# A new order of all steps, and four products with k on GpSimd, in a fused linear-attention and SwiGLU kernel

## The chip, the core and the metric

The kernel runs on one core of one Trainium2 chip. The metric is the device time of one execution in microseconds (us). One profiled execution gives the trace that the numbers below are from.

## What is computed

The first half is a linear attention with a decaying state (RWKV-6), for 4 batches, 8 heads, 768 time steps and head dimension 48; the second a feed-forward part on its output, 3072 rows of 384, with 1536 hidden units.

```
for t in range(S):
    cur = einsum('bhd,bhe->bhde', u * k[t], v[t])
    y[t] = einsum('bhd,bhde->bhe', r[t], state + cur)
    state = w[t][..., None] * state + einsum('bhd,bhe->bhde', k[t], v[t])
x  = y as rows (batch, time) of 384
xn = x / sqrt(mean(x * x) + 1e-6) * rms_g
g  = xn @ w_gate
out = (g * sigmoid(g) * (xn @ w_val)) @ w_out
```

## The kernel before

Time is cut into six blocks n of 128 steps, with four batches j. The order is written out by hand: ORDER is a list of steps `name.n.j`, and the last loop calls the function of each name in that order. Every engine executes its own instructions in the order in which they were called, so ORDER sets the order on TensorE, VectorE, ScalarE, GpSimd and SP's DMA queue at once. What a step waits for on other engines is found from its data.

For a block and a batch, load_w, load_k, load_r and load_v bring 128 x 384 values (L261, SP's queue). ln takes the logarithm of w (ScalarE); cs_mm, for blocks 0 and 1 pcs_mm, adds it up over time with a triangular matrix (TensorE); exp_r and exp_k make exponentials (ScalarE); r_mul and k_mul multiply r and k with them into rk (L471, L477); rk_pe or a DMA transposes it to rkT (rk_tr). q_mm (L518, L520) or pq_mm (L529, L531) multiply r with k, masks cut away the future (q_mask, pmask: VectorE, or a copy by ScalarE and a select by GpSimd), y_mm multiplies with v, st_mm (L575) and st_new bring the state on. The term with u runs on the side: bonus_mul (GpSimd, L483 and L484) makes r k u, bonus_sum (VectorE) its sum per head, bonus_v (GpSimd, L493) times v gives ydiag. x_add adds both. x_sq (ScalarE), x_rstd (GpSimd or ScalarE) and xn_mul (ScalarE, L624) normalize, xn_pe or xn_tr transpose, xn_out multiplies with rms_g.

The feed-forward part takes 512 rows at a time. Blocks 0 and 1 go together as pairs: pgate and pval (L670) work on 256 rows, first those of batch 0, then of batch 1; gate_mm.1 and val_mm.1 (L663) on batches 2 and 3 of the two blocks; gate_mm.2 to gate_mm.5 on blocks 2 to 5 of all batches. A feed-forward group is six matmuls of 256 columns or three of 512; a Silu (ScalarE, table loads at L236) and a product (VectorE) follow it, then o_mm (L720) and out_dma.

The weights w_gate and w_val come in three pieces each, w_out in three: load_gv.g.h (L367; h is 0 for gate, wg_sb_154 to 156 for g of 0 to 2; 1 for val, wv_sb_157 to 159) and load_wo. GpSimd issues them, in its own list between its products, on queue 0 of the DMA; loads of w, k, r and v are on SP's queue 1. pgate.f.0 for f of 0 and 1 uses piece 0, for 2 and 3 piece 1, for 4 and 5 piece 2. PSUM has rings: a and b with two banks each, q with four.

A few sets say which engine does a step: K_POOL (k_mul on GpSimd), CAST_ACT (the cast of v on ScalarE), ODD_COPY (the second mask by ScalarE and GpSimd, not VectorE), RSTD_ACT, EXPR_SB and EXPK_SB (exponentials into SBUF, not PSUM). warm steps are products of zeros on TensorE.

Of the kernel before, what the change touches and what calls it, by code (L numbers as in the profile page):

```python
# [30 lines left out]
pcopy_o.0.0 k_mul.0.1 warm.1.2 rk_pe.0.1 load_w.0.2 ln.0.2 exp_k.1.1 pcs_mm.1.2 load_w.0.3 ln.0.3 pcs_mm.2.2 r_mul.1.1
pmask_e.0.0 k_mul.1.1 rk_pe.1.1 pmask_o.0.0 pmask_o.2.0 pmask_e.2.0 exp_r.1.2 pcs_mm.0.2 exp_k.1.2 load_k.0.2
bonus_sum.1.1 k_mul.1.2 cast_v.0.0 y_mm.1.0 pmask_o.1.0 bonus_v.1.0 x_add.1.0 rk_tr.1.1 load_k.0.3 load_v.0.1
bonus_v.0.0 exp_k.0.2 k_mul.0.2 y_mm.0.0 warm.3.1 x_add.0.0 rk_tr.0.1 pq_mm.3.1 warm.2.2 pcopy_o.3.1 pmask_e.3.1
pq_mm.2.1 pmask_o.2.1 pmask_e.2.1 pcs_mm.1.3 x_sq.1.0 pq_mm.1.1 warm.0.1 x_sq.0.0 load_r.0.2 exp_r.0.2 w_tot.0.2
r_mul.0.2 load_gv.1.0 x_rstd.1.0 pq_mm.0.1 pmask_o.0.1 pmask_e.0.1 pmask_e.1.1 pmask_o.1.1 x_rstd.0.0 bonus_mul.0.1
pmask_o.3.1 load_gv.1.1 xn_mul.1.0 exp_r.1.3 bonus_v.1.1 cast_v.0.1 pcs_mm.0.3 pcs_mm.2.3 rk_pe.0.2 load_gv.0.0
xn_pe.1.0 xn_out.1.0 load_gv.0.1 bonus_sum.0.1 exp_k.1.3 xn_mul.0.0 warm.2.1 xn_pe.0.0 bonus_v.0.1 rk_tr.0.2
xn_out.0.0 y_mm.1.1 x_add.1.1 exp_k.0.3 y_mm.0.1 load_w.2.1 ln.2.1 exp_r.0.3 st_mm.0.1 st_new.0.1 r_mul.1.2 pgate.3.0
st_mm.0.0 st_new.0.0 psilu.3.0 pgate.2.0 psilu.2.0 load_gv.2.0 load_r.0.3 k_mul.0.3 x_add.0.1 r_mul.0.3 x_sq.1.1  # L40
# [10 lines left out]
cs_add.2.1 x_rstd.1.2 pmask_o.1.3 pmask_o.2.3 ln.2.2 xn_mul.1.2 o_mm.0.1 load_w.2.3 load_k.2.0 load_r.2.3 ln.2.0
cs_mm.2.0 x_rstd.0.2 bonus_v.0.3 exp_k.2.1 cs_add.2.0 pmask_o.0.3 exp_k.2.0 bonus_sum.1.3 o_out.0.1 y_mm.0.3 pval.5.1
ph.5.1 pmask_o.3.3 exp_r.2.1 y_mm.1.3 k_mul.2.0 bonus_v.1.3 x_add.0.3 st_mm.0.2 st_new.0.2 load_r.2.1 r_mul.2.1
w_tot.2.1 xn_mul.0.2 x_add.1.3 ln.2.3 exp_r.2.0 w_tot.2.0 o_mm.0.3 xn_pe.0.2 xn_pe.1.2 x_sq.0.3 x_rstd.0.3 o_out.0.3
cs_mm.2.3 xn_out.0.2 cs_add.2.3 load_r.2.0 r_mul.2.0 o_mm.0.0 load_k.2.3 xn_out.1.2 bonus_mul.2.3 load_k.2.1 k_mul.2.1
load_w.3.0 x_sq.1.3 x_rstd.1.3 xn_mul.1.3 load_r.2.2 xn_mul.0.3 load_w.3.1 exp_r.2.3 xn_pe.1.3 cs_mm.2.2 cs_add.2.2
exp_r.2.2 load_v.2.3 exp_k.2.2 rk_tr.2.0 out_dma.0.1 rk_tr.2.1 xn_out.1.3 xn_pe.0.3 xn_out.0.3 load_k.2.2 r_mul.2.2
w_tot.2.2 o_mm.0.2 ln.3.0 exp_k.2.3 r_mul.2.3 w_tot.2.3 ln.3.1 load_v.2.1 val_mm.1.4 gate_mm.1.8 gate_mm.1.3 st_mm.0.3
silu.1.8 o_out.0.0 bonus_mul.2.1 o_out.0.2 silu.1.3 bonus_sum.2.1 st_new.0.3 val_mm.1.8 h_mul.1.8 gate_mm.1.4 silu.1.4
h_mul.1.4 q_mm.2.0 q_mask_e.2.0 q_copy_o.2.0 q_copy_o.2.1 bonus_mul.2.0 cast_v.2.3 k_mul.2.3 q_mask_e.2.1 k_mul.2.2  # L60
# [70 lines left out]
def kernel(  # L131
# [646 lines left out]
```

## Time and profile before

| | us |
|---|---|
| median of 3 runs | 201.34 |
| lowest and highest | 200.47 and 202.33 |
| the profiled execution | 202.45 |
| its span, first to last instruction | 200.6 |
| TensorE's last matmul ends at | 197.3 |

Times in a view count from the first instruction of the span. PE is TensorE, PEld its weight load, DVE VectorE, ACT ScalarE, POOL GpSimd; SPq and POOLq are an engine's sequencer, which issues DMAs. A row of a timeline gives start, duration, engine, line, operation, out<-in and count, and behind `<-` what ended the idle time ahead of it. A row of waits gives the total, the number of waits and the longest one. Durations of successive rows overlap, since engines are pipelined.

### The profile page before, as it was taken

To read this page: it belongs to the slowest core of one execution; us is meant where nothing else is said; L and a number is where in the kernel's file an instruction comes from. 1 tells how busy PE (TensorE), PEld (TensorE's weight loads), DVE (VectorE), ACT (ScalarE), POOL (GpSimd) and SP (SyncE) were. 2 spreads that over 40 slices of the span, in tenths; PEclk is the share of its full clock that TensorE was granted. 3 is DMA by queue.
4 is the path that set the end of the run, shared out by engine and by line. 5 is a ranking of instruction groups with operands and counts; after the bars stand their busy time and mean duration, and the time that the engine had idled before them with its cause. 6 is when DMAs were issued, how large, how long until landed. Compare 5 with 4: busy or idle time off the path is not lost.

```text
span 200.6 us, 4665 instructions
## 1 busy us (share of the span) xinstructions
PE 190.2 (95%) x1708; PEld 120.3 (60%) x1724; DVE 150.6 (75%) x298; ACT 138.9 (69%) x282; POOL 129.3 (64%) x191
## 2 busy tenths in 40 slices
PE   7989968999999989999899999999999999999993
PEld 3556667998765556565456665565655655555562
DVE  5699986979986999998888887798698682154631
ACT  3699996778889448987568986579976665064400
POOL 3599959797399957798879997937696742000000
PEclk9999999999999999999999999999999999999999
DMA  6999999999969899899999768896276002302222
GB/s 160 323 323 233 229 203 194 216 196 212 191 149 203 182 189 207 207 195 180 157 232 202 149 179 177 168 224 132 44 186 141 3 2 59 98 3 78 78 78 78
DMA packets 109886, 32.41 MB, mean 162 GB/s; under 512 B 103972, under 2 KB 109480, under 8 KB 109864
## 3 DMA queue, kind: packets, MB, share of 16 engines
q1 hardware_dynamic: 107024, 28.58, 63.8%
q0 software_dynamic: 2832, 3.54, 10.3%
q8 instruction: 13, 0.21, 0.4%
q14 instruction: 9, 0.07, 0.1%
q10 hardware_dynamic: 8, 0.00, 0.0%
HBM read 25.96 MB, written 4.72 MB: 153 GB/s over the span
## 4 chain that ended last, share of the span: by engine, by line
PE 66%; POOL 13%; DMA 12%; issue 3%; ACT 2%; DVE 1%; SPq 1%; POOLq 0%; DVEq 0%
PE ps_bv L663 8%; PE ps_bu L663 8%; PE ps_au L663 7%; PE ps_av L663 7%; PE ps_qv L720 6%; PE ps_qx L720 5%; PE ps_qu L720 5%; DMA wv_sb<-in_moe_w_val_dram 5%; DMA rkT<-rk 5%; POOL ruk L483 3%; POOL ruk L484 2%; PE ps_qz L720 2%; POOL rk L477 2%; DMA stage_v<-in_v_dram 2%; PE ps_bu L670 2%
## 5 line engine op out<-in xcount | busy, mean ns | idle before, releaser
L720 PEld LDWEIGHTS <-ht 128*128 128x128 bf16 x300 | 28.4, 98 | 17.4 <-DVE ht L706 0.3
L238 ACT ACTIVATE sg<-ps_au 128x512 bf16<-128x512 f32 x35 | 21.0, 599 | 17.2 <-PE ps_au L663 12.9
L238 ACT ACTIVATE sg<-ps_av 128x512 bf16<-128x512 f32 x37 | 22.1, 599 | 12.9 <-PE ps_av L663 10.7
L706 DVE TENSOR_TENSOR ht<-ps_bv,sg 128x512 bf16<-128x512 f32 x30 | 20.6, 687 | 11.5 <-PE ps_bv L663 8.8
L663 PEld LDWEIGHTS <-wg_sb 128*128 128x128 bf16 x180 | 19.3, 114 | 15.8 <-DVE xnt L652 0.2
L663 PEld LDWEIGHTS <-wv_sb 128*128 128x128 bf16 x180 | 19.0, 114 | 15.3 <-DVE xnt L652 0.2
L483 POOL TENSOR_TENSOR ruk<-stage_r,stage_k 128x384 f32<-128x384 f32 x24 | 24.0, 1001 | 4.5 <-DMA stage_r<-in_r_dram 4.4
L484 POOL TENSOR_TENSOR ruk<-ruk,u_bc 128x384 f32<-128x384 f32 x24 | 24.2, 1007 | 2.2 <-POOL ruk L483 0.4
L663 PE MATMUL ps_av<-xnt,wg_sb 128*128 128x512 bf16 x89 | 25.0, 380 | 0.2
L706 DVE TENSOR_TENSOR ht<-ps_bu,sg 128x512 bf16<-128x512 f32 x30 | 20.6, 688 | 5.6 <-PE ps_bu L663 2.9
L663 PE MATMUL ps_bv<-xnt,wv_sb 128*128 128x512 bf16 x85 | 24.1, 380 | 0.3
L663 PE MATMUL ps_bu<-xnt,wv_sb 128*128 128x512 bf16 x86 | 23.9, 380 | 0.4 <-issue 0.2
L663 PE MATMUL ps_au<-xnt,wg_sb 128*128 128x512 bf16 x84 | 23.3, 380 | 0.1
L493 POOL TENSOR_TENSOR ydiag<-stage_v,diag 128x384 f32<-128x384 f32 x24 | 19.8, 832 | 2.0 <-DVE wcol L466 1.0
L477 POOL TENSOR_TENSOR rk<-stage_k,ek 128x384 bf16<-128x384 f32 x16 | 15.9, 1004 | 6.0 <-ACT ek L238 6.0
L720 PE MATMUL ps_qv<-wo_sb,ht 128*128 128x384 bf16 x108 | 19.1, 326 | 0.0
L611 ACT ACTIVATE junk<-xb 128x384 bf16<-128x384 f32 x24 | 12.5, 523 | 5.8 <-DVE xb L606 5.6
L559 POOL TENSOR_SCALAR_AFFINE_SELECT qts<-qts 128x512 bf16<-128x512 bf16 x16 | 10.1, 635 | 8.1 <-ACT qts L556 8.1
L624 ACT ACTIVATE xn<-xb,rstd 128x384 bf16<-128x384 f32 x24 | 14.4, 610 | 1.0 <-POOL rstd L620 0.9
L236 ACT ACT_TABLE_LOAD x10 | 12.8, 1283 | 1.8 <-PEq L762 1.6
L720 PE MATMUL ps_qu<-wo_sb,ht 128*128 128x384 bf16 (+1 forms) x84 | 13.8, 314 | 0.0
L488 DVE TENSOR_REDUCE diag<-ruk 128x8 f32<-128x384 f32 x24 | 13.1, 544 | 0.4 <-POOL ruk L484 0.3
(216 smaller groups left out, 413.5 us busy)
## 6 DMA issues: line engine op xcount, KB each, us to landing
out_dram<-ob SPq DMA_DIRECT2D x23, 192.0 KB, 2.2
stage_w<-in_w_dram SPq DMA_DIRECT2D x16, 192.0 KB, 4.1
stage_k<-in_k_dram SPq DMA_DIRECT2D x16, 192.0 KB, 3.7
stage_r<-in_r_dram SPq DMA_DIRECT2D x16, 192.0 KB, 4.2
stage_v<-in_v_dram SPq DMA_DIRECT2D x16, 192.0 KB, 3.9
stage_w<-in_w_dram SPq DMA_DIRECT2D x4, 384.0 KB, 4.9
stage_k<-in_k_dram SPq DMA_DIRECT2D x4, 384.0 KB, 5.5
stage_r<-in_r_dram SPq DMA_DIRECT2D x4, 384.0 KB, 4.9
```

Of the source, the lines that this page charges most:

```text
L236: nc.scalar.preload_act_table_set(table_name)
L238: return nc.scalar.activation(**kw).ins
L477: eng.tensor_tensor(out=rk[:, n % 2, j, 1, :, 0:D], in0=inp["k", n, j], in1=bank["ek", n, j][:, 0:DM].rearrange("p (h d) -> p h d", h=H), ...
L483: nc.gpsimd.tensor_tensor(out=ruk[n, j], in0=inp["r", n, j], in1=inp["k", n, j], op=ALU.mult)
L484: nc.gpsimd.tensor_tensor(out=ruk[n, j], in0=ruk[n, j], in1=u_bc, op=ALU.mult)
L488: nc.vector.tensor_reduce(out=diag[n, j].rearrange("p h o -> p (h o)"), in_=ruk[n, j], axis=mybir.AxisListType.X, op=ALU.add)
L493: nc.gpsimd.tensor_tensor(out=ydiag[n, j], in0=inp["v", n, j], in1=diag[n, j].to_broadcast([128, H, D]), op=ALU.mult)
L611: nc.scalar.activation(out=junk, in_=xb[n, j], func=AF.Square, accum_out=rstd[n, j][:, 0:1])
L624: nc.scalar.activation(out=xn, in_=xb[n, j], func=AF.Copy, scale=rstd[n, j][:, 1:2])
L663: nc.tensor.matmul(ps, lhsT=units(ws, c, f), rhs=xnt[n][:, c, :], start=(c == 0), stop=(c == KC - 1))
L706: nc.vector.tensor_tensor(out=ht[n][:, f, :], in0=bank.pop(("v", n, f)), in1=bank.pop(("sg", n, f)), op=ALU.mult)
L720: nc.tensor.matmul(ps[:, cols], lhsT=ht[n][:, f, b * L:(b + 1) * L], rhs=wo_sb[:, f, cols], start=(f == 0), stop=(f == FC - 1))
```

## The change

ORDER is another list of the same steps; 9 warm steps where there were 8. Five sets differ. The rest is the same, one line higher up in the file.

```diff
-load_w.0.0 gain_mm.0.0 ln.0.0 pcs_mm.2.0 exp_k.1.0 load_k.0.0 k_mul.1.0 pcs_mm.1.0 u_mm.0.0 exp_r.1.0 exp_k.0.0
+load_w.0.0 ln.0.0 pcs_mm.2.0 exp_k.1.0 load_k.0.0 k_mul.1.0 load_r.0.0 pcs_mm.1.0 exp_r.1.0 r_mul.1.0 u_mm.0.0
...
-    CAST_ACT = sel("02")
-    EXPR_SB = sel("03 13")
-    K_POOL = sel("20 21 22 23 30 31 32 33 40 41 42 43 50 51 52 53")
-    EXPK_SB = sel("13") | K_POOL
+    CAST_ACT = sel("01 02 03")
+    EXPR_SB = sel("02 03 13")
+    K_POOL = sel("02 03 12 13 20 21 22 23 30 31 32 33 40 41 42 43 50 51 52 53")
+    EXPK_SB = K_POOL
...
-    ODD_COPY = sel("00 02 03 10 12 31 32 33")
-    RSTD_ACT = sel("00 02 10 13")
+    ODD_COPY = sel("00 03 12 22 23 32 33")
+    RSTD_ACT = sel("00 10")
```

GpSimd's list around the issues of the weights, before (ydiag is bonus_v, the two lines of ruk are one bonus_mul, CAST vp is cast_v, rstd is x_rstd):

```order
L493 TENSOR_TENSOR ydiag<-stage_v,diag 128x384 x2
L367 DMA wg_sb_155<-in_moe_w_gate_dram 128x3x512
L483 TENSOR_TENSOR ruk<-stage_r,stage_k 128x384
L484 TENSOR_TENSOR ruk<-ruk,u_bc 128x384
L547 AFFINE_SELECT qts<-qts 128x512
L367 DMA wv_sb_158<-in_moe_w_val_dram 128x3x512
L493 TENSOR_TENSOR ydiag<-stage_v,diag 128x384
L408 CAST vp<-stage_v 128x768
L367 DMA wg_sb_154<-in_moe_w_gate_dram 128x3x512
L367 DMA wv_sb_157<-in_moe_w_val_dram 128x3x512
L493 TENSOR_TENSOR ydiag<-stage_v,diag 128x384
L367 DMA wg_sb_156<-in_moe_w_gate_dram 128x3x512
```

The same place now, which begins behind two bonus_mul:

```order
L366 DMA wg_sb_154<-in_moe_w_gate_dram 128x3x512
L482 TENSOR_TENSOR ruk<-stage_r,stage_k 128x384
L483 TENSOR_TENSOR ruk<-ruk,u_bc 128x384
L407 CAST vp<-stage_v 128x768
L546 AFFINE_SELECT qts<-qts 128x512
L492 TENSOR_TENSOR ydiag<-stage_v,diag 128x384 x2
L366 DMA wv_sb_157<-in_moe_w_val_dram 128x3x512
L366 DMA wg_sb_155<-in_moe_w_gate_dram 128x3x512
L366 DMA wv_sb_158<-in_moe_w_val_dram 128x3x512
L366 DMA wg_sb_156<-in_moe_w_gate_dram 128x3x512
L476 TENSOR_TENSOR rk<-stage_k,ek 128x8x48
```

Piece 0 now goes first, its gate half ahead of a bonus product, and four issues stand together; the last line is one of the four products with k that moved here.

ScalarE's list around the first Silu, before (er and ek are exp_r and exp_k, lw is ln of block 2, rkT is rk_tr, xn is xn_mul, sg is a Silu, junk is x_sq):

```order
L238 ACTIVATE er<-ps_bv 128x384
L238 ACTIVATE ek<-ps_av 128x384
L624 ACTIVATE xn<-xb,rstd 128x384
L509 COPY rkT<-ps_qx 128x1024
L238 ACTIVATE ps_bv<-ps_bv 128x384
L238 ACTIVATE lw<-stage_w 128x8x48
L238 ACTIVATE er<-ps_au 128x388
L236 ACT_TABLE_LOAD
L238 ACTIVATE sg<-ps_av 128x512
L238 ACTIVATE sg<-ps_au 128x512
L611 ACTIVATE junk,rstd<-xb 128x384
L509 COPY rkT<-ps_qv 128x1024
```

The same place now:

```order
L623 ACTIVATE xn<-xb,rstd 128x384
L237 ACTIVATE ek<-ps_au 128x384
L237 ACTIVATE er<-ps_av 128x388
L237 ACTIVATE lw<-stage_w 128x8x48
L237 ACTIVATE ek<-ps_bv 128x384
L235 ACT_TABLE_LOAD
L237 ACTIVATE sg<-ps_au 128x512
L237 ACTIVATE sg<-ps_av 128x512
L405 CAST vp<-stage_v 128x768
L508 COPY rkT<-ps_qv 128x1024
L508 COPY rkT<-ps_qz 128x1024
L610 ACTIVATE junk,rstd<-xb 128x384
```

The copy of rkT that stood ahead of the Silus stands behind them, and so does a cast of v, batch 1, which was GpSimd's.

SP's list of loads, from the fifth on, before (128x8x96 is a pair of blocks, 128x8x48 one block):

```order
L261 DMA stage_r<-in_r_dram 128x8x96
L261 DMA stage_k<-in_k_dram 128x8x96
L261 DMA stage_v<-in_v_dram 128x8x96
L261 DMA stage_w<-in_w_dram 128x8x96 x2
L261 DMA stage_k<-in_k_dram 128x8x96 x2
L261 DMA stage_v<-in_v_dram 128x8x96
L261 DMA stage_r<-in_r_dram 128x8x96
L261 DMA stage_w<-in_w_dram 128x8x48
```

And now:

```order
L260 DMA stage_r<-in_r_dram 128x8x96
L260 DMA stage_w<-in_w_dram 128x8x96
L260 DMA stage_k<-in_k_dram 128x8x96
L260 DMA stage_v<-in_v_dram 128x8x96
L260 DMA stage_w<-in_w_dram 128x8x96
L260 DMA stage_k<-in_k_dram 128x8x96
L260 DMA stage_r<-in_r_dram 128x8x96
L260 DMA stage_w<-in_w_dram 128x8x48
L260 DMA stage_v<-in_v_dram 128x8x96 x2
L260 DMA stage_r<-in_r_dram 128x8x96
L260 DMA stage_k<-in_k_dram 128x8x96
L260 DMA stage_v<-in_v_dram 128x8x96
```

The second v (batch 1) was twelfth and is thirteenth, behind w of block 2; k of batch 3 was eleventh and is sixteenth.

More of the change, by code (lines that the diff above doesn't have):

```diff
@@ L31 @@
[L31 to L40, printed above, removed]
@@ L51 @@
[L51 to L60, printed above, removed]
@@ new lines @@
+pcopy_o.0.0 pq_mm.1.0 k_mul.0.1 pcs_mm.1.2 warm.0.0 exp_r.1.2 exp_k.0.2 r_mul.0.1 rk_pe.0.1 pmask_e.0.0 k_mul.1.1
+pcs_mm.0.2 rk_pe.1.1 warm.2.2 warm.3.2 bonus_sum.0.0 load_v.0.0 load_w.0.3 ln.0.3 rk_tr.0.1 cast_v.0.0 pmask_e.1.0
+pmask_o.0.0 pmask_o.1.0 y_mm.1.0 st_mm.0.0 bonus_v.1.0 bonus_v.0.0 x_add.1.0 load_gv.0.1 exp_r.0.2 y_mm.0.0 pcs_mm.2.3
+st_new.0.0 x_add.0.0 rk_tr.1.1 pq_mm.3.1 pmask_e.3.1 pq_mm.1.1 pmask_e.1.1 pcs_mm.0.3 warm.5.2 x_sq.1.0 exp_k.1.3
+x_rstd.1.0 pq_mm.0.1 pmask_o.3.1 x_sq.0.0 load_gv.1.0 pmask_e.0.1 x_rstd.0.0 load_k.0.2 load_r.0.2 xn_mul.0.0
@@ new lines @@
+pq_mm.0.3 pcopy_o.0.3 cast_v.0.3 bonus_sum.0.3 bonus_v.0.3 pmask_e.0.3 pmask_o.0.3 xn_mul.0.2 pq_mm.1.3 pgate.5.1
+psilu.5.1 pmask_o.2.3 pmask_o.1.3 bonus_sum.1.3 pmask_e.1.3 ln.2.0 pval.0.1 ph.0.1 o_mm.0.1 o_out.0.1 y_mm.0.3
+x_add.0.3 load_v.2.1 x_rstd.1.2 xn_mul.1.2 cs_mm.2.1 cs_add.2.1 exp_k.2.1 exp_r.2.1 st_mm.0.2 y_mm.1.3 bonus_v.1.3
+xn_pe.0.2 cs_mm.2.0 x_add.1.3 w_tot.2.1 st_new.0.2 x_sq.1.3 ln.2.3 r_mul.2.1 x_sq.0.3 xn_out.0.2 cs_add.2.0 ln.2.2
+ph.5.1 o_mm.0.0 o_out.0.0 xn_pe.1.2 xn_out.1.2 exp_r.2.0 r_mul.2.0 x_rstd.0.3 xn_mul.0.3 x_rstd.1.3 xn_mul.1.3
@@ new lines @@
+st_new.3.3 gate_mm.2.8 silu.2.8 val_mm.2.6 h_mul.2.6 ln.4.1 val_mm.2.8 h_mul.2.8 bonus_mul.4.2 load_v.4.1 bonus_v.3.2
+x_add.3.2 x_sq.3.2 load_w.4.2 ln.4.2 cs_mm.4.0 xn_pe.3.0 xn_out.3.0 cs_add.4.0 exp_r.4.0 exp_k.4.0 bonus_mul.4.0
+load_v.5.1 load_r.5.2 x_rstd.3.3 cast_v.4.3 out_dma.1.0 bonus_sum.4.0 w_tot.4.0 x_rstd.3.2 xn_mul.3.2 xn_mul.3.3
+o_mm.2.1 o_out.2.1 cs_mm.4.1 cs_add.4.1 exp_k.4.1 exp_r.4.1 k_mul.4.0 cast_v.5.1 o_mm.2.0 r_mul.4.0 cs_mm.4.2
+xn_pe.3.1 cs_add.4.2 load_k.4.1 load_r.4.3 k_mul.4.1 load_k.4.3 xn_pe.3.2 xn_out.3.2 w_tot.4.1 load_k.5.2 load_r.4.1
@@ new lines @@
+r_mul.4.1 o_mm.2.2 xn_out.3.1 bonus_mul.4.3 exp_r.4.2 w_tot.4.2 r_mul.4.2 ln.4.3 o_out.2.0 cs_mm.4.3 cs_add.4.3
+exp_k.4.3 bonus_v.4.0 k_mul.4.3 bonus_sum.4.2 exp_r.4.3 exp_k.4.2 out_dma.2.1 out_dma.1.1 xn_pe.3.3 xn_out.3.3
+r_mul.4.3 cast_v.4.2 st_mm.4.0 st_new.4.0 o_out.2.2 k_mul.4.2 ln.5.3 w_tot.4.3 o_mm.2.3 o_out.2.3 gate_mm.3.6 silu.3.6
+val_mm.3.4 val_mm.3.6 h_mul.3.6 rk_tr.4.0 gate_mm.3.3 silu.3.3 rk_tr.4.1 q_mm.4.0 q_mask_e.4.0 q_copy_o.4.1
+q_mask_e.4.1 load_w.5.0 gate_mm.3.4 silu.3.4 cast_v.4.1 load_k.5.3 bonus_sum.4.3 bonus_v.4.2 val_mm.3.3 gate_mm.3.5
@@ new lines @@
+x_add.4.1 x_sq.4.1 h_mul.3.9 load_r.5.0 xn_tr.4.0 y_mm.4.3 x_add.4.3 silu.3.0 gate_mm.3.1 val_mm.3.0 h_mul.3.0
+x_rstd.4.1 xn_mul.4.1 x_sq.4.3 silu.3.1 val_mm.3.5 h_mul.3.5 gate_mm.3.7 load_k.5.0 val_mm.3.1 x_rstd.4.2 xn_mul.4.2
+h_mul.3.1 x_rstd.4.3 xn_mul.4.3 val_mm.3.8 h_mul.3.8 load_r.5.3 bonus_mul.5.2 silu.3.7 ln.5.0 st_mm.4.2 cs_mm.5.3
+val_mm.3.7 h_mul.3.7 o_mm.3.1 cs_add.5.3 st_new.4.2 cs_mm.5.0 cs_add.5.0 exp_r.5.3 ln.5.1 r_mul.5.3 exp_k.5.3 o_mm.3.2
+out_dma.2.0 load_v.5.3 xn_tr.4.1 exp_r.5.0 r_mul.5.0 load_w.5.2 ln.5.2 bonus_mul.5.0 cast_v.5.0 bonus_mul.5.1
@@ new lines @@
+x_sq.5.0 x_rstd.5.2 xn_mul.5.2 val_mm.4.11 xn_mul.5.3 h_mul.4.11 xn_tr.5.3 val_mm.4.2 h_mul.4.2 out_dma.3.1 xn_tr.5.2
+gate_mm.4.7 x_add.5.1 silu.4.7 val_mm.4.7 h_mul.4.7 gate_mm.4.10 x_rstd.5.0 silu.4.10 out_dma.3.0 val_mm.4.10
+h_mul.4.10 o_mm.4.0 o_mm.4.2 x_sq.5.1 x_rstd.5.1 xn_mul.5.0 xn_mul.5.1 o_mm.4.1 xn_tr.5.0 o_mm.4.3 xn_tr.5.1
+xn_gain.5.1 xn_gain.5.2 xn_gain.5.0 gate_mm.5.4 silu.5.4 gate_mm.5.7 silu.5.7 val_mm.5.7 val_mm.5.4 o_out.4.1
+o_out.4.0 gate_mm.5.9 silu.5.9 o_out.4.3 gate_mm.5.2 h_mul.5.4 silu.5.2 out_dma.4.0 val_mm.5.2 h_mul.5.2 gate_mm.5.5
@@ new lines @@
+gate_mm.5.6 h_mul.5.7 silu.5.5 val_mm.5.5 h_mul.5.5 val_mm.5.9 h_mul.5.9 silu.5.6 out_dma.4.3 gate_mm.5.10 silu.5.10
+gate_mm.5.0 silu.5.0 val_mm.5.0 h_mul.5.0 gate_mm.5.3 out_dma.4.1 gate_mm.5.1 silu.5.1 val_mm.5.1 h_mul.5.1 val_mm.5.6
+h_mul.5.6 gate_mm.5.8 silu.5.3 val_mm.5.3 h_mul.5.3 silu.5.8 val_mm.5.10 h_mul.5.10 gate_mm.5.11 silu.5.11 o_out.4.2
+val_mm.5.8 h_mul.5.8 out_dma.4.2 val_mm.5.11 h_mul.5.11 o_mm.5.0 o_out.5.0 out_dma.5.0 o_mm.5.1 o_mm.5.4 o_out.5.4
+out_dma.5.4 o_out.5.1 o_mm.5.2 out_dma.5.1 o_out.5.2 o_mm.5.3 o_out.5.3 out_dma.5.2 out_dma.5.3
```

144 lines of the change are left out of this document (64 added, 80 removed).

## The prediction

> **What bounds the kernel now.** I read the page first (busy times, then the chain of work that ended last), then the busy times by stretch, TensorE's own waits, and last the timelines of single engines in the first 60 us.
>
> ```profile
> span 200.6 us, 4665 instructions
> PE 190.2 (95%) x1708; PEld 120.3 (60%) x1724; DVE 150.6 (75%) x298; ACT 138.9 (69%) x282; POOL 129.3 (64%) x191
> PE 66%; POOL 13%; DMA 12%; issue 3%; ACT 2%; DVE 1%; SPq 1%; POOLq 0%; DVEq 0%
> ```
>
> The 95% is an average. The stretches, and TensorE's waits over the whole span, tell where it is soft:
>
> ```profile
> 0.00:22.40 22.40, 20.39 (x223) 11.84 (x224) 17.79 (x49) 17.50 (x35) 16.44 (x29) 1.00 0.99 250
> 22.40:34.60 12.20, 9.93 (x142) 8.36 (x141) 10.13 (x19) 10.26 (x20) 9.71 (x14) 1.00 1.20 218
> 34.60:60.00 25.40, 25.40 (x309) 21.01 (x307) 22.16 (x45) 20.83 (x46) 19.68 (x28) 1.00 0.98 193
> 110.00:197.30 87.30, 86.70 (x623) 50.84 (x630) 57.66 (x106) 53.96 (x113) 41.84 (x64) 1.00 0.44 106
> 197.30:200.60 3.30, 0.00 (x1) 0.00 (x0) 0.36 (x1) 0.00 (x0) 0.00 (x0) 0.99 0.25 89
> ...
> PE ps_bu L670 <- DMA wv_sb<-in_moe_w_val_dram: 2.0, 2, 1.5
> PE ps_qu L518 <- DMA rkT<-rk: 0.7, 1, 0.7
> PE ps_qz L575 <- POOL rk L477: 0.4, 1, 0.4
> PE ps_qv L518 <- DMA rkT<-rk: 0.4, 1, 0.4
> PE ps_qx L518 <- DMA rkT<-rk: 0.4, 1, 0.4
> ```
>
> The columns after each stretch's length are PE, PEld, DVE, ACT, POOL. From 34.6 to 197.3 TensorE has no gap but about 1.9 us (0.7 and three of 0.4); its work there cannot shrink by a new order. The last 3.3 us are the output's copy and DMA, built alike in both orders. So the time is set by how much of TensorE's work is behind it by about 34 us. In that stretch it waits 2.0 us for a weight, and before it, it fills time with small products and warm-up products on zeros. Its rows there:
>
> ```profile
> 24.98 0.82 PE L670 MATMUL ps_av<-xnt,wg_sb 128*128 128x256 bf16 x6
> 29.09 0.85 PE L670 MATMUL ps_bu<-xnt,wv_sb 128*128 128x256 bf16 x6 [1.53 <-DMA wv_sb<-in_moe_w_val_dram]
> 33.98 0.84 PE L670 MATMUL ps_bu<-xnt,wv_sb 128*128 128x256 bf16 x6 [0.50 <-DMA wv_sb<-in_moe_w_val_dram]
> 38.51 0.66 PE ps_bv L670 x6
> ```
>
> The first feed-forward group (six matmuls, 0.65 us of TensorE each by the chain's row) starts at 24.98. The one at 33.98 is the seventh; six are done by then.
>
> **The weights.** GpSimd issues the weights in its own order, among its products; queue 0 delivers them in that order:
>
> ```profile
> 16.91 0.98 POOL L367 DMA_DIRECT2D wg_sb<-in_moe_w_gate_dram  x1
> 20.55 0.81 POOL L367 DMA_DIRECT2D wv_sb<-in_moe_w_val_dram  x1
> 22.92 0.80 POOL L367 DMA_DIRECT2D wg_sb<-in_moe_w_gate_dram  x1
> 23.72 0.77 POOL L367 DMA_DIRECT2D wv_sb<-in_moe_w_val_dram  x1
> ...
> DMA to landing us min/median/max: 7.2/8.5/11.1
> ...
> DMA to landing us min/median/max: 8.5/10.1/10.2
> ```
>
> (The last two rows are the landings of wg_sb and of wv_sb.) The piece issued at 20.55 lands at about 29.05, that of 23.72 at 33.9; one piece lies between them, so a queue with work brings a piece each 2.45 us. In the new order (GpSimd's rows in the section on the change) wg_sb_154 goes out behind two bonus products, long before it is wanted. wv_sb_157 takes about the place that the piece of 16.91 had: ahead of it stand the same three bonus products, cast and two ydiag, one select less (0.6) and one issue more (0.8), so 17.1. Three more issues follow at once, 0.8 apart. The first lands after the shortest time above, 7.2 us, at 24.3; the next at 26.8, 29.2 and 31.7, 2.45 apart; the sixth, issued near 24.8 behind two products with k and a bonus product, comes next in the queue at 34.1.
>
> **The first group.** ScalarE works step behind step ahead of it, so the first group comes when ScalarE has scaled both blocks of batch 0:
>
> ```profile
> 12.28 0.51 ACT L238 ACTIVATE ps_bv<-ps_bv 128x384 f32<-128x384 f32 x1
> 12.69 0.62 ACT L540 CAST qts<-ps_qz 128x512 bf16<-128x512 f32 x1
> 22.50 0.61 ACT L624 ACTIVATE xn<-xb,rstd 128x384 bf16<-128x384 f32 x1
> 26.52 0.60 ACT L238 ACTIVATE sg<-ps_av 128x512 bf16<-128x512 f32 x1
> ```
>
> (An exponential, a copy, the second block's scaling and the first Silu; steps overlap, so an exponential holds ScalarE 0.4 and a copy 0.5.) Ahead of the second scaling the new order has two copies and one exponential less: 22.5 - 1.4 = 21.1, and I add 0.3 for waits on the sums over x. Then 0.6 for the scaling and about 0.8, an estimate, for the transposes and VectorE's gain: 22.8. (Before, 2.5 us lay between 22.50 and 24.98, since VectorE did other steps between; with all of that the start would be 23.9, the far end, and the gain 1.1 less.) Behind it TensorE's list, 0.65 for each group and the small products between, gives 24.6 for the first use of wv_sb_157, 27.2 for wg_sb_155, 29.1 for wv_sb_158, 31.7 for wg_sb_156 and 34.6 for wv_sb_159, against landings of 24.3, 26.8, 29.2, 31.7 and 34.1. That is 0.2 us of waiting at most in place of 2.0; the thirteenth group starts at 34.8. At 34.8 twelve groups are done, where before had six at 33.98; of the small products the two lists differ by then by one rk transpose less and a q and an xn transpose more, which cancel. Gain: 6 x 0.65 - (34.8 - 33.98) = 3.1 us.
>
> **The other edits.**
>
> ```profile
> L477 POOL TENSOR_TENSOR rk<-stage_k,ek x16: 993/999/1048, 52.3 to 147.3; 128x384 bf16<-128x384 f32 x16
> L477 DVE TENSOR_TENSOR rk<-stage_k,ps_bv x3: 544/544/544, 13.1 to 26.7; 128x384 bf16<-128x384 f32 x3
> L408 POOL CAST vp<-stage_v x3: 819/829/833, 14.0 to 43.3; 128x768 bf16<-128x768 f32 x3
> L406 ACT CAST vp<-stage_v x1: 877/877/877, 36.8 to 36.8; 128x768 bf16<-128x768 f32 x1
> L544 DVE TENSOR_TENSOR qts<-ps_qv,mask_lt x2: 681/681/681, 22.9 to 49.9; 128x512 bf16<-128x512 f32 x2
> L547 POOL TENSOR_SCALAR_AFFINE_SELECT qts<-qts x8: 624/632/639, 13.4 to 48.4; 128x512 bf16<-128x512 bf16 x8
> L620 POOL TENSOR_TENSOR rstd<-rstd,mhalf x20: 547/548/570, 28.5 to 167.2; 128x1 f32<-128x1 f32 x20
> ```
>
> Four products with k go from VectorE to GpSimd (4 x 1.0 against 4 x 0.54), two casts of v from GpSimd to ScalarE (2 x 0.83 against 2 x 0.88), two rstd from ScalarE to GpSimd (about 0.75 each with the short scalar step ahead), one mask less is selected on GpSimd (0.63) and done by VectorE (0.68) without ScalarE's copy. GpSimd gains 4.0 + 1.5 - 1.7 - 0.6 = 3.2 us, VectorE loses 1.5, ScalarE changes by less than 1. From 22.4 to 60 GpSimd is busy 29.4 of 37.6 us, so 3.2 more fit; I cost them at nothing. If that cover is gone, it shows at k's products of batch 3: by GpSimd's list with these durations they end near 37.2 and 38.2, and TensorE wants them at 38.0 and 38.4; each us that GpSimd is late there is a us of the gain. One more warm-up step (two products, 0.3) lies where TensorE waits anyway. The gain's product (gain_mm) leaves the start of TensorE's list: up to 0.2 earlier, or nothing.
>
> **The loads.** They ride on SP's queue, over the same 16 DMA engines as the weights:
>
> ```profile
> 4.40 1.15 SPq L261 DMA_DIRECT2D stage_r<-in_r_dram  x1
> 14.09 2.53 SPq L261 DMA_DIRECT2D stage_r<-in_r_dram  x1
> 53.34 1.59 SPq L261 DMA_DIRECT2D stage_v<-in_v_dram  x1
> ...
> stage_v<-in_v_dram SPq DMA_DIRECT2D x16, 192.0 KB, 3.9
> stage_k<-in_k_dram SPq DMA_DIRECT2D x4, 384.0 KB, 5.5
> stage_v<-in_v_dram SPq DMA_DIRECT2D x4, 384.0 KB, 13.5
> ```
>
> Alone, loads follow each other by 1.2 us. The pair loads of k, mostly before the weights, land in 5.5 us; those of v, mostly among them, in 13.5. The new order puts v of batch 1 behind w of block 2 (rows on SP): it is the thirteenth load. The thirteenth was issued at 14.09; with the first weight now among the early loads I put it at 16. It lands between 21.5 (5.5 later) and 29.5 (13.5 later), and ScalarE's cast wants it at 25.4. I take 25, no wait, because it is first in line when the weights' queue fills near 20; at the far end ScalarE would stand 4.1 us, which is kept for the range: 3.1 - 0.7 - 4.1 is 1.7 us slower, 203.0. [...]
>
> **The sum.** Profiled execution: 202.45 us with a span of 200.6, so 1.85 lies around it; it stands 0.55% above the median of 201.34. From 34.8, TensorE needs what before needed from 33.98 less 3.9: 163.3 - 3.9 = 159.4, ending at 194.2; with the 3.3 of the tail 197.5. The new order has more places with no slack (above, and in the second rival), and I allow two waits of about 0.35, the size of those for rkT: 0.7. Gain 3.1 - 0.7 = 2.4 us; ends: 3.8 (no new wait, and the longest rkT wait gone) and, below nothing, the second rival. 202.45 - 2.4 = 200.05 for the profiled execution, 198.9 for the median.
>
> **Rivals.**
>
> First, the weights' lead is paid by the loads. For it: 13.5 against 5.5. Then v of batch 1 lands near 26.4, ScalarE stands 1 us at the cast, and both copies of rkT and x's sums behind it come 1 us late; k of batch 3, now the sixteenth load where it was the eleventh, costs 0.6 more at GpSimd's products with k. Against it: a pause in the weights between 34 and 36, since wo_sb is issued only near 33. Gain 3.1 - 0.7 - 1.6: 200.5.
>
> Second, slower: the load queue becomes the bound at 57 to 62 us. The last v that the first state products of block 2 need was the thirtieth load, issued at 53.34 and landed 3.9 later at 57.2; now it is the thirty-third, with loads of block 3 ahead, so about 60.2 at one load per us. Its cast ends at 60.7, TensorE wants it at 60.9. If the three loads take 2.5 us each, it lands at 64.7 and TensorE waits 4.3: 203.2. It is slower than before from a landing at 63.3 on. For it: GpSimd's casts also stand behind it. Against: in before the queue had room from 56 on.
>
> Third, the change does not do what it says: the first group still starts near 25 because x's sums come late, and only the wait for the weights goes: gain 0.5, 200.8.
>
> **How the numbers follow.** Forecast 0.47 (197.5 to 199.8), first rival 0.25, second 0.20, third 0.08. One per cent, about what a measurement can tell, is 2.0 us. Faster by over 1% (under 199.3) is most of the forecast: 0.44. Slower (over 203.4) is most of the second rival: 0.17. Within 1%: 0.39. The range 197.5 to 203.2 leaves out 0.03 below and 0.16 above: its low end is the sum's own, its high end the second rival's price, with the far end of the load of v inside.
>
> **What would show it.** Right: a first group near 22.8, no wait for wv_sb over 0.5, the thirteenth group before 35.5, the last o_mm ending near 195. Wrong: ScalarE idle before the cast of v near 25 (first rival), TensorE waiting at L574 or GpSimd at L407 for stage_v near 60 (second), a first group after 24.5 (third), or GpSimd's rstd ending after 53 for batch 3, which would hold the second feed-forward part at 56.5.

## The result, and the profile after

The changed kernel takes 200.06 us (median of 20 runs, 197.99 to 204.31) where the kernel before takes 201.39 beside it (20 runs, 200.47 to 202.36). Its executions fall into two groups of ten: 197.99 to 198.96, with 198.5 in the middle, and 201.16 to 204.31, and the profiled one (202.48 us, span 200.6) is of the second. The ratio to the kernel before, from executions of the first group, is 0.986 (0.984 to 0.988): 2.9 us faster; the medians of all 20 runs differ by 1.3. The forecast was 198.9, 197.5 to 203.2. What parts the two groups is the main question below.

The page of the changed kernel, its span, busy times and the chain that ended last:

```profile
span 200.6 us, 4677 instructions
PE 189.7 (95%) x1710; PEld 120.2 (60%) x1726; DVE 151.4 (75%) x295; ACT 138.5 (69%) x279; POOL 132.6 (66%) x196
PE 79%; DMA 9%; DVE 3%; ACT 2%; issue 2%; POOL 2%; SPq 0%; DVEq 0%; POOLq 0%
```

POOL has gained 3.3 us, as worked out. The chain holds more of PE (79 for 66%) and less of POOL (2 for 13%). The stretches after, columns as before:

```profile
22.40:34.60 12.20, 9.48 (x139) 8.17 (x138) 9.43 (x18) 9.29 (x18) 8.58 (x13) 1.00 1.20 222
34.60:60.00 25.40, 23.16 (x297) 19.54 (x297) 23.08 (x40) 19.85 (x41) 19.80 (x29) 1.00 0.93 188
110.00:197.30 87.30, 86.86 (x625) 50.92 (x632) 57.43 (x107) 53.70 (x110) 42.61 (x65) 1.00 0.42 102
```

TensorE is no busier from 22.4 to 34.6 than it was (9.48 for 9.93), and has lost 2.2 us behind it, where it had no gap. Its waits over the whole span say why:

```profile
PE ps_qu L591 <- ACT vp L405: 2.3, 1, 2.3
PE ps_bv L669 <- DVE ht L687: 2.2, 1, 2.2
PE ps_qu L306 <- DVE still L304: 1.0, 1, 1.0
PE ps_qu L634 <- ACT xn L623: 0.2, 1, 0.2
```

The weights are gone from this list, and so are the four waits for rkT and rk that cost 1.9 us before (the 1.0 is the start of the program). In their place stand two new ones. The first, in the timelines of ScalarE, GpSimd and TensorE:

```profile
28.24 0.83 ACT L405 CAST vp<-stage_v 128x768 bf16<-128x768 f32 x1 [2.30 <-DMA stage_v<-in_v_dram]
...
28.36 1.61 POOL L492 TENSOR_TENSOR ydiag<-stage_v,diag 128x384 f32<-128x384 f32 x2 [3.20 <-DMA stage_v<-in_v_dram]
...
29.12 0.56 PE L591 MATMUL ps_qu<-vp,qts 128*128 128x48 bf16 x16 [2.26 <-ACT vp L405]
```

This is v of batch 1, the thirteenth load: three engines stand for it at once. The second wait comes from VectorE and GpSimd:

```profile
37.56 0.68 DVE L535 TENSOR_TENSOR qts<-ps_qu,mask_le 128x512 bf16<-128x512 f32 x1
38.16 3.85 DVE L470 TENSOR_TENSOR rk<-stage_r,er 128x384 bf16<-128x384 f32 x1
41.93 0.68 DVE L687 TENSOR_TENSOR ht<-ps_bv,sg 128x512 bf16<-128x512 f32 x1
...
37.66 0.86 POOL L492 TENSOR_TENSOR ydiag<-stage_v,diag 128x384 f32<-128x384 f32 x1
38.45 1.23 POOL L546 TENSOR_SCALAR_AFFINE_SELECT qts<-qts 128x512 bf16<-128x512 bf16 x2
39.65 1.94 POOL L476 TENSOR_TENSOR rk<-stage_k,ek 128x384 bf16<-128x384 f32 x2
41.54 0.60 POOL L372 DMA_DIRECT2D wo_sb<-in_moe_w_out_dram  x1
```

A product with r that takes 0.55 us elsewhere lasts 3.85: it starts inside a ydiag of GpSimd and ends half a microsecond after GpSimd turns to a DMA issue at 41.54. Of the four GpSimd operations behind the ydiag, two are products with k that the change moved there. Both waits together are 4.5 us, and TensorE's last matmul ends at 197.3, as before. Without them, as an estimate, it would end at 192.8 and the span be 196.1; the spans of the first group are 196.1 to 197.1.

### The profile page after: what moved, and what is told of

The parts are those of the page before. It is cut to its first block, busy times and chain, and to the rows that moved or that the text cites. A ratio compares the mean times of both kernels' runs of the same rounds, so it can differ in the third digit from the quotient of the medians.

```text
span 200.6 us, 4677 instructions
## 1 busy us (share of the span) xinstructions
PE 189.7 (95%) x1710; PEld 120.2 (60%) x1726; DVE 151.4 (75%) x295; ACT 138.5 (69%) x279; POOL 132.6 (66%) x196
## 3 DMA queue, kind: packets, MB, share of 16 engines
q1 hardware_dynamic: 107024, 28.58, 62.2%
q0 software_dynamic: 2832, 3.54, 10.5%
## 4 chain that ended last, share of the span: by engine, by line
PE 79%; DMA 9%; DVE 3%; ACT 2%; issue 2%; POOL 2%; SPq 0%; DVEq 0%; POOLq 0%
PE ps_av L662 11%; PE ps_bu L662 10%; PE ps_bv L662 9%; PE ps_au L662 9%; PE ps_qx L719 9%; DMA stage_v<-in_v_dram 7%; PE ps_qz L719 5%; PE ps_qv L719 5%; PE ps_qu L719 4%; DMA stage_w<-in_w_dram 2%; PE ps_bu L669 1%; PE ps_bv L669 1%; PE ps_qz L517 1%; DVE rk L470 1%; DVE ht L687 1%
## 5 line engine op out<-in xcount | busy, mean ns | idle before, releaser
L237 ACT ACTIVATE sg<-ps_au 128x512 bf16<-128x512 f32 x35 | 20.9, 596 | 21.4 <-PE ps_au L662 13.3
L662 PEld LDWEIGHTS <-wg_sb 128*128 128x128 bf16 x180 | 19.5, 114 | 16.7 <-DVE xnt L651 0.4
L662 PE MATMUL ps_av<-xnt,wg_sb 128*128 128x512 bf16 x93 | 25.9, 380 | 0.2
L662 PE MATMUL ps_bv<-xnt,wv_sb 128*128 128x512 bf16 x82 | 23.4, 379 | 0.3
L662 PE MATMUL ps_au<-xnt,wg_sb 128*128 128x512 bf16 x82 | 22.6, 380 | 0.2
L476 POOL TENSOR_TENSOR rk<-stage_k,ek 128x384 bf16<-128x384 f32 x20 | 20.2, 1017 | 1.0 <-ACT ek L237 0.9
L719 PE MATMUL ps_qx<-wo_sb,ht 128*128 128x384 bf16 x108 | 19.0, 326 | 0.0
L619 POOL TENSOR_TENSOR rstd<-rstd,mhalf 128x1 f32<-128x1 f32 x22 | 12.1, 550 | 1.8
```

What stands on the lines that cost most here:

```text
L237: return nc.scalar.activation(**kw).ins
L476: eng.tensor_tensor(out=rk[:, n % 2, j, 1, :, 0:D], in0=inp["k", n, j], in1=bank["ek", n, j][:, 0:DM].rearrange("p (h d) -> p h d", h=H), ...
L662: nc.tensor.matmul(ps, lhsT=units(ws, c, f), rhs=xnt[n][:, c, :], start=(c == 0), stop=(c == KC - 1))
L719: nc.tensor.matmul(ps[:, cols], lhsT=ht[n][:, f, b * L:(b + 1) * L], rhs=wo_sb[:, f, cols], start=(f == 0), stop=(f == FC - 1))
```

## Experiments

The question was first what parts the groups (the late load, VectorE's product, or something else), then what each part of the change is worth. Places in the order are steps of `ORDER`.

**The changed kernel again, twice** (no edit).

> The changed kernel as it is, for a second profile beside the first one, whose span was 200.6 us. In the first profile TensorE waited 2.3 us at L591 for a cast whose load of v landed at 28.2, and 2.2 us at L669 behind a product with r on VectorE that lasted 3.85 us in place of 0.55. If both waits are fixed parts of the new order, the second profile shows them again and a span near 200.6. [...]

> The changed kernel as it is, once more beside the next one, for a profile of one of its shorter executions. If the load of v of batch 1 is what splits its times, a profile with a span near 196.5 shows this load landing by about 26 and no wait over 1 us at L591; with a span near 200.5 or more it shows it after 27 and a wait of 2 us or more there.

The first took 203.61 us (one run; the kernel before beside it 202.80). The other took 203.02 in the median (kernel before beside it: 201.75): 2 of its 12 executions are in the first group, 198.37 and 198.96, and one is an outlier of 1088. So the first group's share is not fixed, 10 of 20 and then 2 of 12, and in that second measurement the changed kernel is slower in the median. Both profiles are of the longer kind, and neither has the wait at L669. TensorE's waits over 0.3 us behind the start are one in each, of the first and then of the second:

```profile
PE ps_qu L591 <- ACT vp L405: 4.8, 1, 4.8
```

```profile
PE ps_qu L591 <- ACT vp L405: 4.2, 1, 4.2
```

v of batch 1 landed at 30.7 and 30.2. VectorE's long product is not needed for a long execution; the late load was in all three. No profile of an execution of the first group came, so what this load does there is not seen directly; kernels below show the order with this load early.

**v of batch 1 earlier; r's product earlier; both.** Three kernels: the first hunk alone, the second alone, both.

```diff
+load_v.0.1
 load_k.0.2
...
-load_v.0.1
```
```diff
+r_mul.1.3
 pmask_e.1.2
...
-r_mul.1.3
```

> The changed kernel with the load of v of batch 1 three places earlier on the load queue, ahead of k, r of batch 2 and w of block 2; nothing else moves. The changed kernel's times fall into two groups, near 198.5 and near 202.5 us, and two profiles of the second group show ScalarE idle 2.3 and 4.8 us before the cast of this v, which landed at 28.2 and 30.7. Theory of the load (the first rival of the prediction): this v, issued beside the weights, is the coin that falls one way or the other; issued near 10.5 it lands before 20, the wait at L591 is gone in every execution, and the times are one group near 198.5, lowest no lower than 197.5. [...]

> The changed kernel with r's product of batch 3 for the upper block three steps earlier in VectorE's order, where GpSimd issues two weight transfers instead of running selects and products; nothing else moves. In one profile this product, which reads two operands from SBUF, lasted 3.85 us while GpSimd ran two selects and two products with k back to back, and TensorE waited 2.2 us. [...] Theory of the load alone: the median and both groups as before, 198.5 and 202.5.

> The changed kernel with both edits: v of batch 1 three places earlier on the load queue, and r's product of batch 3 three steps earlier on VectorE. [...] If only the load matters, the same as with the load's move alone, within 0.3. If something else splits the times, two groups stay.

None did away with the second group: 202.77 (198.37 to 206.41), 203.38 (198.47 to 203.99) and 204.48 us (199.15 to 206.85), six runs each. In the second kernel the wait at L591 stood again (5.0 us): r's product is not what parts the groups. In the first, v landed at 17.5, and w of block 2, now thirteenth, took its place. ScalarE in that kernel:

```profile
22.17 0.49 ACT L237 ACTIVATE er<-ps_av 128x388 f32<-128x388 f32 x1
28.33 0.52 ACT L237 ACTIVATE lw<-stage_w 128x384 bf16<-128x384 f32 x1 [5.66 <-DMA stage_w<-in_w_dram]
28.76 0.47 ACT L237 ACTIVATE ek<-ps_bv 128x384 f32<-128x384 f32 x1
29.25 1.28 ACT L235 ACT_TABLE_LOAD   x1
30.54 0.60 ACT L237 ACTIVATE sg<-ps_au 128x512 bf16<-128x512 f32 x1
```

That w was issued at 14.0 and landed at 28.3: 14.3 us for half the bytes of a pair load. So the late load is not one particular load; what makes it late is its place in the queue. The expectation for the load's theory was wrong there.

**Nothing wanted early in the bad place.** w of block 2, batch 1, is loaded with the other w of block 2, and its logarithm (ScalarE) goes to the others.

```diff
-load_w.2.1 ln.2.1
...
+load_w.2.1
 load_w.2.0
...
+ln.2.1
 ln.2.0
```

> The changed kernel with w of block 2, batch 1, loaded with the other w of block 2 (after the pair loads), and its logarithm moved likewise to the others on ScalarE; v of batch 1 so becomes the twelfth load, issued near 12.9, with 192 KB less ahead of it. Moving v ahead of w had only changed which load stood in the bad place (w then landed at 28.3 and ScalarE stood 5.7 us). Theory of the place: the first load that is issued when the weights' transfers pile up (from 17 on) takes 13 to 15 us; with nothing wanted early in that place the wait at L591 goes down to 0 to 1 us, the upper group of times vanishes, median 198 to 199, against two groups at 198.5 and 202.5. Rival: the slower executions have another cause and the waits only follow it; then two groups stay, as with the two earlier edits of the load queue.

One group: 199.02 us (197.78 to 199.84, 6 runs), 0.987 (0.983 to 0.992) of before. v of batch 1, now twelfth, lands at 21.3, and v of batch 2, now thirteenth, takes 16.1 us and harms nobody: it lands at 31.0, and its cast begins at 34.1 with no wait for it:

```profile
34.11 0.83 ACT L405 CAST vp<-stage_v 128x768 bf16<-128x768 f32 x1
```

This moved only one load and one logarithm, and the profiled execution (199.84) is one in which the load that the table below goes by landed late. So the late load is shown to be what makes the second group.

**The same, and one cumulative sum later.** The logarithm, now behind ScalarE's table load, held TensorE for 0.4 us in that kernel.

```diff
-cs_mm.2.1 cs_add.2.1 exp_k.2.1 exp_r.2.1
 st_mm.0.2
 y_mm.1.3
 bonus_v.1.3
+cs_mm.2.1 cs_add.2.1 exp_k.2.1 exp_r.2.1
```

> The changed kernel with w of block 2, batch 1, and its logarithm late, as in the earlier run whose median was 199.0 us, and with the cumulative sum of this batch a few steps later on TensorE, behind y of batch 3. In that run TensorE stood 0.4 us for the logarithm at 48.7, and 1.3 us in three places later on. If the 0.4 is a loss by itself: median 198.4 to 198.8, one group of times. If the later waits come from a bound of their own (loads and GpSimd near 90 us) that takes back whatever is won earlier: 198.8 to 199.2, no change from that run.

198.43 us (198.09 to 199.01, 5 runs), 0.987 (0.985 to 0.990) of the 201.15 of before beside it: as good as the changed kernel's first group, with no run in a second one. Its profile shows what the changed order does when its loads come in time. TensorE's waits over the whole span:

```profile
PE ps_qu L306 <- DVE still L304: 1.0, 1, 1.0
PE ps_qu L634 <- ACT ob L728: 0.2, 1, 0.2
PE ps_au L669 <- ACT ek L237: 0.2, 1, 0.2
PE ps_qz L634 <- ACT xn L623: 0.2, 1, 0.2
```

And its stretch from 22.4 (11.93 us busy of 12.20, where the kernel before had 9.93), with the first and the thirteenth group of TensorE's timeline:

```profile
22.40:34.60 12.20, 11.93 (x170) 10.62 (x169) 11.76 (x23) 11.52 (x22) 11.57 (x16) 1.00 1.19 221
```

```profile
23.41 0.82 PE L669 MATMUL ps_au<-xnt,wg_sb 128*128 128x256 bf16 x6 [0.18 <-ACT ek L237]
...
35.39 0.82 PE L669 MATMUL ps_bu<-xnt,wv_sb 128*128 128x256 bf16 x6
```

**What the thirteenth load does, over all profiles.** In every profile with early weights, the landing of the tenth load (issued between 10.1 and 10.5, beside the first weight transfer) tells which load will be late:

| kernel | tenth load lands | thirteenth lands | fourteenth lands |
|---|---|---|---|
| cumulative sum later | 15.1 | 22.0 | 31.1 |
| w out, products back (below) | 15.1 | 22.6 | 31.0 |
| early weights alone (below) | 15.1 | 21.7 | 29.5 |
| products back (below) | 16.8 | 27.3 | 33.5 |
| both moves | 17.3 | 28.1 | 33.3 |
| v earlier | 17.5 | 28.3 | 33.7 |
| changed kernel | 17.6 | 28.2 | 33.3 |
| r's product earlier | 18.2 | 30.8 | 34.1 |
| early weights, w out of the way (below) | 18.7 | 29.5 | 34.4 |
| changed kernel, first repeat | 18.8 | 30.7 | 34.0 |
| w out | 18.9 | 31.0 | 34.5 |
| changed kernel, second repeat | 19.3 | 30.2 | 34.3 |

Where the tenth lands at 15.1, the thirteenth still slips through by 22.6 and the fourteenth is the first late one; where it lands at 16.8 or after, the thirteenth is. In the changed kernel the thirteenth is v of batch 1, wanted at 25.4, and the fourteenth is v of batch 2, wanted near 34. By this its first group are the executions in which the tenth lands early; that is inferred from the other kernels, since no profile of the changed kernel fell into that group.

The packets in the traces show where the two cases part. Those of the first weight piece begin between 13.7 and 14.5 us and run to about 17. In the three profiles with 15.1, no packet of SP's queue starts between 14.8 and 15.9; in the nine others 13 to 173 do. So the tenth load seems to have all its packets under way by 14.8, or to end among the weight's packets; what decides that stays open.

**The weights late again.** The changed kernel with its six transfers at about the times of the kernel before (GpSimd's steps only).

```diff
-load_gv.0.0
 bonus_mul.0.1
...
 bonus_v.0.0
+load_gv.0.0
...
 bonus_mul.1.1
+load_gv.0.1
 k_mul.1.2
+load_gv.1.0 load_gv.1.1
...
 bonus_v.1.1
+load_gv.2.0
...
 bonus_mul.0.2
+load_gv.2.1
```

> The changed kernel with its six weight transfers issued about when the kernel before issued them (near 17, 21, 23, 24, 25.5 and 29 us, between the same products on GpSimd); all else as changed. This undoes the weights' edit alone. Theory of the weights (the prediction's main term): the second piece lands near 29 and TensorE, which wants it at 25, waits 3 to 4 us; time 201 to 203 with one group, since v of batch 1 then has the queue to itself and lands before 24. Rival: if the gain came from the order of the computing steps and not from the weights, the time stays within 0.5 of 198.5 (lower group).

202.84 us (201.81 to 204.03, 12 runs), one group, 1.007 (1.003 to 1.010) of before: 4.3 more than the 198.5 of the changed kernel's first group, and about what its second group takes. v landed at 19.7, and TensorE waits in one place:

```profile
PE ps_bv L669 <- DMA wv_sb<-in_moe_w_val_dram: 3.1, 1, 3.1
```

Behind this wait TensorE's granted clock is lower too, 0.86 from 22.4 to 34.6 (the last section comes back to it). The new order has no gain without the early weights, and its late v comes from them.

**The early weights alone, and with w out of the way.** The kernel before with its transfers at the new places (first behind the second bonus product, four behind ydiag, the last behind the next bonus product); the second kernel has `load_w.2.1` and `ln.2.1` moved to the others of block 2 as well.

```diff
 bonus_mul.0.0
+load_gv.1.0
...
 bonus_v.0.0
+load_gv.1.1 load_gv.0.0 load_gv.0.1 load_gv.2.0
...
 bonus_mul.0.1
+load_gv.2.1
```

> The kernel before with its six weight transfers issued at the places of the changed kernel (near 11, 17, 18, 18.5, 19 and 23 us), in its own order of pieces; all else as before. Theory of the weights: the waits of 2.0 us for wv_sb go; if nothing else is late the time is 199.2 to 199.6. Theory that the weights' lead is paid by the loads: v of batches 0 and 1 (landing 24 to 32 and 41 before) lands 2 or more us later and gives the gain back, 201 or more, or splits the times into two groups. If the first group of the feed-forward part is what the search moved, the weights alone bring at most 2.0 of the 2.9 us.

> The kernel before with its weights issued at the changed kernel's places, which alone made it 208.4 us with ScalarE standing 4.5 us for w of block 2, and now with this w and its logarithm moved to the other ones of block 2. If that load in the bad place was the loss, most of it comes back: 200.5 to 203. If the new waits of TensorE there (2.6 us for products with r, 1.7 for v's cast) come from the whole queue being late and not from this one load, the time stays at 205 or more: then the weights' lead can only be used with a new order of loads.

208.36 us (206.65 to 209.12, 6 runs; 1.033, 1.028 to 1.038) and 205.71 (204.30 to 212.10, 7 runs; 1.021, 1.018 to 1.024). No wait for a weight is left in either. (The landings of 32 and 41 that the first expectation gives to v of batches 0 and 1 are those of batches 2 and 3; v of batch 1, the twelfth load, landed at 19.0 in the kernel before.) In the first kernel, w of block 2 is fourteenth and the late one:

```profile
29.56 0.52 ACT L238 ACTIVATE lw<-stage_w 128x384 bf16<-128x384 f32 x1 [4.45 <-DMA stage_w<-in_w_dram]
```

The only profile of the second kernel is of its longest execution (212.1; the six others are 204.3 to 205.9), so it shows the kind of wait and not its price in a usual execution. The tenth load, a k, landed at 18.7 and already held VectorE there (the 2.5 below); the late one is the thirteenth, a load of r, at 29.5:

```profile
PE ps_av L419 <- DVE rk L471: 5.5, 1, 5.5
PE ps_au L273 <- DVE rk L477: 2.5, 1, 2.5
PE ps_au L431 <- ACT lw L238: 1.1, 1, 1.1
```

So the same six transfers cost the old order 7 us and bring the new one 4.3 in its first group. Clearing one load gives back 2.7 of the 7 and does not mend it, as the rival said: in that profile the load that came next into the place was wanted early too (VectorE stood for it from 22.7).

**The four products with k back on VectorE**, in the changed kernel, and in the kernel with w out of the early loads.

```diff
-K_POOL = sel("02 03 12 13 20 21 22 23 30 31 32 33 40 41 42 43 50 51 52 53")
-EXPK_SB = K_POOL
+K_POOL = sel("20 21 22 23 30 31 32 33 40 41 42 43 50 51 52 53")
+EXPK_SB = sel("02 03 12 13") | K_POOL
```

> The changed kernel with its four additional products with k back on VectorE (from the same tiles in SBUF, in the same places of the order); this undoes that edit alone. The prediction costed the edit at nothing, hidden beside other work: then the times are the same within 0.3 us in both groups. [...] If the edit is what the gain came from, the median goes to 200.5 or more.

> The changed kernel with w of block 2, batch 1, out of the early loads (which left one group of times, median 199.0) and the four additional products with k back on VectorE as well. The prediction costed the products' move at nothing: then 198.7 to 199.3. With them back on VectorE beside the late load the median was 201.7, with waits of 0.7 and 0.6 us of TensorE's k transposes for VectorE; if that is the price of the products by itself, and not of the load, 200.3 to 201.7 here, with the same waits for the transposes at L499 and none at L591.

201.73 us (200.22 to 205.51, 6 runs) and 200.42 (200.19 to 201.47, 12 runs; 0.995, 0.992 to 0.997). In the second, TensorE waits for no late load: it is 1.4 us above the 199.02 with the products on GpSimd. TensorE's waits there, and VectorE's and GpSimd's rows:

```profile
PE ps_qx L499 <- DVE rk L476: 0.7, 1, 0.7
PE ps_qu L499 <- DVE rk L476: 0.5, 1, 0.5
```

```profile
38.96 2.45 DVE L476 TENSOR_TENSOR rk<-stage_k,ek 128x384 bf16<-128x384 f32 x2
...
38.67 1.06 POOL L492 TENSOR_TENSOR ydiag<-stage_v,diag 128x384 f32<-128x384 f32 x1 [0.45 <-DVE diag L487]
39.70 1.30 POOL L482 TENSOR_TENSOR ruk<-stage_r,stage_k 128x384 f32<-128x384 f32 x1
41.08 1.20 POOL L483 TENSOR_TENSOR ruk<-ruk,u_bc 128x384 f32<-128x384 f32 x1
```

Two products on VectorE take 2.45 us where 1.1 was counted, and GpSimd's beside them 1.30 and 1.20 where their mean in the changed kernel is 1.0; TensorE wants their transposes at once. In the first kernel VectorE's product with r was long as well: 37.22 to 39.16, again from inside a ydiag to just behind a DMA issue (38.69).

The other edits of the change (the casts, the rstd steps, the masks, the exponentials into SBUF, gain_mm and the warm-up step) were not undone one by one; what each is worth is not shown.

## Why the prediction was right, and where it was not

**The weights: right.** Landings were forecast at 24.3, 26.8, 29.2, 31.7 and 34.1; in the profile after they are 22.4, 26.3, 28.9, 31.5 and 34.2. No wait for wv_sb is left where 0.2 was allowed. With the weights late again 4.3 us are lost, 3.1 of them as a wait: this was the term that carries. The first landing was 1.9 early, and nothing hung on it, since TensorE wants that piece at 24.94.

**The first group: right in kind, 0.4 to 0.6 us late.** It starts at 23.18, and at 23.41 in the kernel without late loads, not at 22.8. ScalarE was in time (the second scaling at 21.4 to 21.6, where 21.4 was forecast); the 0.8 us for what comes behind it measured 1.2, with small products of TensorE between and 0.2 of waiting (in the kernel without late loads for an exponential that reads the PSUM buffer). The thirteenth group carries this on: 35.39 for 34.8.

**The sum: the allowance had the wrong sign.** I took off 0.7 us for new waits. In the kernel without late loads there were none, and the old waits for rkT and rk, 1.9 us, went too. From its thirteenth group to its last matmul (192.95) TensorE takes 157.6 us; 159.4 less 1.9 is 157.5. Against the profiled execution of before that makes 3.1 - 0.6 + 1.9 = 4.4 us, and 202.45 - 198.09 is 4.4. In the medians measured side by side it is 2.7 (201.15 to 198.43), since the profiled execution of before lay 1.3 above that median and this one 0.3 below its own.

**The median of the first group: near by luck in part.** For the profiled execution I forecast 200.05, and without late loads it is 198.09: 2.0 too high, from the 0.7 and the 1.9 less the 0.6 above. For the median I forecast 198.9, only 0.4 over the first group's 198.5, because I took 1.1 off for the distance between profile and median, and in the new order that distance is not there (0.3, the other way).

**The load of v: wrong in the executions of the second group,** 10 of 20 and most of the repeat. The step that failed is "I take 25, no wait, because it is first in line when the weights' queue fills near 20". It was issued at 14.0 to 15.6, earlier than the 16 that I put, and landed at 28.2, 30.2 and 30.7, around the far end of 29.5 and beyond it. In the profiles, being first in line helped only where the tenth load had landed at 15.1: there the thirteenth came at 22, better than I put it. In the other executions the first rival's mechanism holds, at a higher price: in the three profiles TensorE loses 2.3, 4.2 and 4.8 us there, not 1. A single landing time between the two ends was the mistake; the load takes one end or the other. The median of all 20 runs, 200.06, inside the range, is a mix of the two groups that no term of the sum stands for.

**The products with k: not nothing.** "I cost them at nothing" came from GpSimd's room. On VectorE they cost 1.4 us in the new order, since TensorE wants their transposes sooner than VectorE makes them: the two of batch 3 take 2.45 us there beside GpSimd's products. Part of this is paid back where VectorE's product with r lasts 3.85 us beside GpSimd's operations, 2.2 us of waiting in one profile of the three.

**The second and third rivals** did not happen: TensorE has no wait for anything behind 60 us in the profile after, and its first group is not at 25. (In the second, the landing from which the kernel would be slower should read 62.8 by the prediction's own terms: 60.9 less the cast's 0.5 plus the gain of 2.4.) One sign of being wrong came without what it stood for: rstd of batch 3 ended at 59.0, and at 54.7 without late loads, past the 53 named, but the second feed-forward part began at 62.2 and 57.9, with no wait for it, and not at 56.5.

## What to carry to other kernels

Where two DMA queues fill at once, find the first loads behind that moment, and see to it that nothing wanted soon stands there; moving the urgent v ahead here only put w into the place, which landed at 28.3. An early transfer is worth what the order around it can bear: the same six issues were worth 4.3 us in one order, in the executions whose loads came in time, and cost 7 in another. When a kernel's times form two groups, look for a wait that comes and goes before trusting a median or the one profiled execution.

## What the hardware showed that was not expected

- **From one load to the next, the time to land doubled.** Pair loads of w, all issued ahead of the weights in the kernel before, take 4.9 us in the median. The first that meets the weights took 13.4 to 16.7 us for 384 KB and 11.9 to 14.3 for 192 KB, while the ones just ahead took 7 to 9. Where the thirteenth was the first, the one behind it took 15.0 to 15.7, and was wanted only near 34 in the changed kernel. The issue itself stretched: two loads took 4.9 us on SP, in the kernel with the cumulative sum later, where one takes 1.15.

```profile
12.71 4.89 SPq L260 DMA_DIRECT2D stage_v<-in_v_dram  x2
```

Which load is the first late one goes with a spread of 4 us in the landing of a load that is always issued within 0.4 us, beside the first weight transfer. What sets that spread stays open; a later first transfer was not tried.
- **A product on VectorE lasted through several operations of GpSimd.** Twice in the new order a product with r of two SBUF operands that started inside a ydiag lasted until GpSimd went to a DMA issue (3.85 and 1.94 us for 0.55). Two more took 1.25, and the other products with r of batch 3 in the new order 0.54 to 0.94. During the first, GpSimd ran four operations behind that ydiag, from 38.45 to 41.54. The cause was not tested by itself.
- **Waits of 3 to 5 us came with a lower granted clock.** In the second repeat of the changed kernel TensorE's granted clock from 22.4 to 34.6 is 0.77, with a wait of 4.2 us in it, and the first feed-forward group behind the wait takes 1.46 us; in the first profile, with a wait of 2.3 us and a clock of 1.00, the same group takes 0.83. The stretch and the group in the second repeat:

```profile
22.40:34.60 12.20, 7.71 (x102) 6.46 (x101) 6.28 (x13) 6.88 (x12) 6.78 (x9) 0.77 1.19 232
...
32.34 1.46 PE L669 MATMUL ps_au<-xnt,wg_sb 128*128 128x256 bf16 x6
```

The 4.8 us in the first repeat went with 0.89. With the weights late again, the listed wait of 3.1 us went with 0.86, and the stretch from 28.4 to 31.8 behind it ran at 0.50. That the waits lowered the clock, and from what length on, is not shown.
